# Mixture of experts after attention: a third expert's early product, early weights by columns, a later routing chain

## The chip, the cores and the metric

One core of one Trainium2 chip. The metric is the device time of one execution in microseconds, the median of repeated runs. TensorE multiplies, VectorE and ScalarE work elementwise, GpSimd issues the indirect scatters, and SyncE (SP) issues the other transfers.

## What is computed

```
q_pool = q.reshape(B, H, S // 2, 2, D).mean(axis=3)        # 4, 8, 1152, 64
attn   = softmax(q_pool @ k^T / sqrt(D));  x = attn @ v     # 2304 tokens x 512
logits = x @ w_gate;  noisy = logits + log1p(exp(x @ w_noise)) * noise
top2   = two largest of 8 experts per token, softmax weights over the two
for e in range(8):  h = relu(x[mask] @ w1[e]);  out[mask] += w * (h @ w2[e])
```

w1[e] is 512 x 1024 and w2[e] is 1024 x 512, in float32.

## The kernel before

**Precision.** Every float32 operand of the experts is split into two fp16 parts, a high and a low one, and a product is three matmuls: high by high, low by high, high by low. A 512 KB piece of a weight (four pieces for each of w1[e] and w2[e]) comes into one of four raw buffers (`qr`, `kn`, `kr`, `vr`). `split` (L907) makes the high part on ScalarE (L918) and the low part on VectorE (L920). `load` (L895) then brings the next piece into a raw buffer.

**Stages.** First comes attention, until about 446 us, in two halves of the heads' groups. Tokens of the first half are routed during it and scattered by expert into `xg` in device memory (640 rows at most are computed for each expert). Then comes the **early stage** (`Moe.early`, L1000): for experts 0 and 1 the first 256 rows, which hold tokens of the first half alone, go through both products while the second half's tokens are still being routed. Then comes the **main part** (`Moe.run`, L1049): the other 384 rows of experts 0 and 1 and all 640 of experts 2 to 7, with each expert's second product behind the next one's first. Main needs the rows of the second half, loaded from `xg` by a transposing transfer (`xload`, L925).

**The two products.** `mm1` (L956) is the first: for each of eight column blocks f, 12 matmuls of N columns (256 early, 384 or two times 320 in main) into a PSUM tile `pss`. There are two such tiles, `pss_63` and `pss_64`, and early products use a half of one each, so a pair of f shares a tile. ScalarE makes `hh` of it (L1015 early, L980 main) and VectorE the lower half `hl` (L1019, L981). `mm2` (L983) is the second: for each block of 128 rows 24 matmuls of 512 columns (L988).

**The routing chains.** For a group of three token blocks, transposed rows `xTg` are multiplied by the gate weights (logits, L693). Then a long chain of small VectorE steps on tiles `rt` and `ru` (L696 to L800) picks the two experts. A rank product on TensorE (L803 to L806) counts tokens per expert, a few VectorE steps make row addresses, and GpSimd scatters (L97). In the early stage there are two: chain C (tiles `rtc`, `ruc`) for group 0, six scatters, and chain A (`rta`, `rua`) for groups 1 and 2 together, twelve scatters.

**What sets the order.** `Plan` emits the program in the order of a simulated schedule: each operation has a key (about its due time in us), a cost, dependences and buffers, and of those that can start it takes one by start and key. `route` (L572) gives a chain's steps keys that grow by `pace`. Expert e's early work has keys from LATE + 23 e, where LATE is 440.

Of the kernel before, what the change touches and what calls it, by code (L numbers as in the profile page):

```python
# [19 lines left out]
P = 128  # L20
# [8 lines left out]
E = 8  # L29
# [7 lines left out]
NEARLY = 2  # L37

# [179 lines left out]
class Attn:  # L218
# [307 lines left out]
    def others(s, F0, out):  # L526
# [91 lines left out]
class Route:  # L618
    def __init__(s, tc, ctx, B, wg, wn, noise):
        s.tc, s.nc, s.B = tc, tc.nc, B  # L620
        nc = s.nc
        s.per = B.const
        s.rp = ctx.enter_context(tc.tile_pool(name="rt", bufs=1))
        s.wk = ctx.enter_context(tc.tile_pool(name="rwk", bufs=3))
        s.dram = ctx.enter_context(tc.tile_pool(name="rdram", bufs=1, space=DRAM))
        s.xg = s.dram.tile([E * FULL, XW], U16, name="xg")
        s.A, s.C = ("a", 9, 14, 6), ("c", 3, 18, 8)
        s.group, s.xr, s.pre = [], {}, {}
        for g in range(3):
            s.xr[1, g] = s.rp.tile([P, 3, XW], F16, name=f"xr{g}")  # L630
        s.args = wg, wn, noise
# [48 lines left out]
    def logits(s, j, g, L, gap, last):  # L680
        nc = s.nc
        xr = s.xr[j, g]
        xT = []
        for c in range(3):
            xT.append(s.rp.tile([P, 8, P], F16, name="xTg", bufs=6))
# [180 lines left out]
class Moe:  # L866
    def __init__(s, tc, ctx, B, R, F0, w1, w2, out):
# [3 lines left out]
        s.x = pool("mx", 2)  # L871
# [22 lines left out]
    def load(s, eng=None):  # L894
# [5 lines left out]
        r = s.B.flat(s.F0.raws[(s.nl - 1) % 4])  # L900
        if nm == "1":
            eng.dma_start(r, s.w1[e, c * P:(c + 1) * P])
        else:
            eng.dma_start(r.rearrange("p (a f) -> p a f", a=2),
                                s.w2[e, 2 * c * P:2 * (c + 1) * P].rearrange("(a p) f -> p a f", p=P))
        s.pre[e, nm, c] = r

    def split(s, e, nm, c, half=None, load=True):
        nc = s.nc
        if c == 0 and half != 1:  # L910
            if nm == "1" and e % 2 == 0:
# [44 lines left out]
    def mm1(s, e, f, a=0, b=CAP, ps=None):  # L956
# [3 lines left out]
        if e not in s.H:  # L960
            s.H[e] = tuple(s.h.tile([P, 8, CAP], F16, name=f"h{x}") for x in "hl")
# [41 lines left out]
    def early(s, A):  # L1003
# [4 lines left out]
        s.W[0, "1"] = s.F0.w  # L1008
        fl, ld, done = {}, {}, {}
# [15 lines left out]
        for x, (e, nm) in enumerate(((0, "2"), (1, "1"), (1, "2"))):  # L1025
            for c in range(4):
                key = LATE + (2, 12, 24)[x] + (2, 2.5, 2.5)[x] * c
                hi = op("ACT", 1.06, key, lambda e=e, nm=nm, c=c: s.split(e, nm, c, 0), deps=[ld[x, c]] if x else ())
                lo = op("DVE", 1.14, key, lambda e=e, nm=nm, c=c: s.split(e, nm, c, 1, False), deps=[hi])
                last = ld[x + 1, c] = op("SP", 0.6, key, s.load, deps=[lo], lat=5.0, after=last)  # L1030
                done.setdefault((e, nm), []).append(lo)
# [17 lines left out]
    def run(s):  # L1049
        s.nc.gpsimd.tensor_copy(s.B.sp, s.X[0, EARLY][0:1, 7, CAP - EARLY - 1:CAP - EARLY])  # L1050
        s.put()
        for e in range(E + 1):
            if e < E:
                s.meta(e, EARLY if e < NEARLY else 0, CAP)
                for f in range(8):
                    s.mm1(e, f, EARLY if e < NEARLY else 0, CAP)
                    s.flush()
                    if 1 <= e < E - 1:
                        s.split(e + 1, "1", f // 2, f % 2)
                if 1 <= e < E - 1:  # L1060
                    s.xload(e + 1, 0, CAP)
# [150 lines left out]
```

## Time and profile before

| | before |
|---|---|
| median of 3 runs | 891.49 us (889.52 to 892.16) |
| profiled execution | 896.5 us, span 894.6 us |
| mean granted TensorE clock | 0.962 |
| TensorE matmul busy | 819.0 us (92%) |
| VectorE / ScalarE / GpSimd busy | 534.6 / 445.0 / 402.6 us |
| DMA, whole span | 137.80 MB, mean 154 GB/s |

The profile is of one execution, 5.0 us longer than the median of the runs; its span leaves out 1.9 us around it. Matmuls are pipelined: a matmul's own duration is longer than the distance to the next one, so throughput is read from starts and counts. The granted clock is the share of TensorE's full clock that it was given.

### The profile page before, as it was taken

The page shows a single profiled execution, that of the slowest core. Times are in us where ns is not written, and L with a number is a line of the kernel's source. Part 1 is how long each engine was busy: PE and PEld are TensorE (multiplying, and loading weights), DVE is VectorE, ACT ScalarE, POOL GpSimd, SP SyncE. Part 2 cuts the span into 40 slices and gives each one's busy share as a digit, 9 for nine tenths or more (in the row PEclk, how much of TensorE's full clock was granted, in tenths as well). Part 3 has the DMA queues.
Part 4 walks back from the last instruction along what each step waited for, and adds up shares of the span by engine and source line. Part 5 has one row for each costly group of instructions (what it writes and reads, how often), then busy time and mean ns, then how long its engine had stood idle before and what let it go on. Part 6 is the DMA issues. An engine that isn't in the chain of part 4 may idle for free.

```text
span 894.6 us, 21128 instructions
## 1 busy us (share of the span) xinstructions
PE 819.0 (92%) x8685; PEld 537.1 (60%) x8685; DVE 534.6 (60%) x1226; ACT 445.0 (50%) x662; POOL 402.6 (45%) x389
## 2 busy tenths in 40 slices
PE   3889999999999877899988899999999999999995
PEld 1546777767767655677766365756475655647542
DVE  4877898899889988899887142434233241422200
ACT  4658888777878465586543132333233232322310
POOL 4447879887996867664633312020201102020222
PEclk9989999999999779899989899999999999999998
DMA  8899796898999587664586826282827346291143
GB/s 194 166 238 211 181 231 176 200 200 194 194 214 203 116 183 189 169 172 110 122 215 231 205 55 147 82 214 71 217 68 201 84 126 158 72 219 18 24 52 45
DMA packets 213637, 137.80 MB, mean 154 GB/s; under 512 B 150304, under 2 KB 183584, under 8 KB 213536
## 3 DMA queue, kind: packets, MB, share of 16 engines
q1 hardware_dynamic: 204896, 116.33, 53.6%
q0 software_dynamic: 8640, 20.08, 11.0%
q8 instruction: 69, 1.13, 0.5%
q14 instruction: 32, 0.26, 0.1%
HBM read 62.14 MB, written 35.44 MB: 109 GB/s over the span
## 4 chain that ended last, share of the span: by engine, by line
PE 64%; DVE 20%; issue 4%; ACT 4%; DMA 3%; another core or an unknown queue 1%; SPq 1%; POOL 1%; ACTq 0%; DVEq 0%; POOLq 0%
PE pss L971 23%; PE psm L988 21%; PE psm L385 7%; PE psm L304 5%; PE pss L350 4%; DVE pl L362 4%; PE pss L349 4%; DVE rd L318 3%; DVE kd L298 1%; ACT rd L312 1%; ACT pf L357 1%; DVE vv L288 1%; DVE mx L327 1%; DMA qt<-qn 1%
## 5 line engine op out<-in xcount | busy, mean ns | idle before, releaser
L365 POOL TENSOR_TENSOR pl<-pf 128x384 f16<-128x384 f32 x288 | 279.9, 1002 | 95.6 <-ACT pf L357 70.9
L357 ACT ACTIVATE pf<-pss 128x768 f32<-128x768 f32 x216 | 174.2, 813 | 72.1 <-PE pss L350 59.1
L97 POOL DMA_INDIRECT out_dram<-y,mti x40 | 62.2, 1554 | 317.4 <-ACT y L993 311.8
L385 PEld LDWEIGHTS <-pf 128*128 128x128 bf16 x2880 | 159.6, 99 | 52.8 <-issue 23.7
L385 PE MATMUL psm<-vv,pf 128*128 128x65 f16 (+1 forms) x2880 | 169.9, 196 | 6.0 <-ACT rd L312 3.2
L385 PE MATMUL psm<-vv,pl 128*128 128x65 f16 (+1 forms) x1440 | 161.1, 195 | 4.5 <-DVE pl L362 2.9
L349 PE MATMUL pss<-qt,kt 128*128 128x384 f16 (+1 forms) x576 | 152.1, 293 | 5.6 <-ACT pf L357 5.4
L350 PE MATMUL pss<-qt,kt 66*128 66x384 f16 (+1 forms) x576 | 152.6, 294 | 0.4 <-DMA qt<-qn 0.4
L981 DVE SCALAR_TENSOR_TENSOR hl<-pss,hh 128x640 f16<-128x640 f32 (+1 forms) x64 | 48.5, 758 | 158.9 <-ACT hh L980 158.9
L385 PEld LDWEIGHTS <-pl 128*128 128x128 f16 x1440 | 128.6, 100 | 6.1 <-DVE pl L362 3.4
L988 PE MATMUL psm<-wh,hh 128*128 128x512 f16 x320 | 122.5, 383 | 3.8 <-ACT hh L1015 3.8
L988 PE MATMUL psm<-wh,hl 128*128 128x512 f16 x320 | 122.3, 382 | 0.5 <-issue 0.5
L988 PE MATMUL psm<-wl,hh 128*128 128x512 f16 x320 | 122.5, 383 | 0.1
L318 DVE CUSTOM_DVE_ANT_0 rd<-psm,rd 128x512 f32<-128x512 f32 x144 | 97.3, 684 | 25.4 <-ACT rd L312 21.0
L988 PEld LDWEIGHTS <-hh 128*128 128x128 f16 x640 | 62.9, 98 | 79.8 <-ACT hh L1015 4.6
L993 ACT ACTIVATE y<-psm,mg 128x512 f32<-128x512 f32 x40 | 27.5, 688 | 152.0 <-issue 77.3
L980 ACT ACTIVATE hh<-pss 128x640 f16<-128x640 f32 (+1 forms) x64 | 41.7, 652 | 122.9 <-PE pss L971 122.9
L312 ACT ACTIVATE rd<-psm 128x512 f32<-128x512 f32 x144 | 85.9, 597 | 24.6 <-PE psm L304 19.7
L304 PE MATMUL psm<-kt,qt 128*128 128x512 f16 (+3 forms) x320 | 79.8, 325 | 16.4 <-DVE mx L318 8.7
L971 PE MATMUL pss<-xT,fh 128*128 128x320 f16 (+1 forms) x448 | 83.4, 303 | 0.0
L971 PE MATMUL pss<-xT,wh 128*128 128x320 f16 (+1 forms) x448 | 83.4, 303 | 0.0
L362 DVE TENSOR_TENSOR pl<-pf 128x768 f16<-128x768 f32 x72 | 82.0, 1151 | 0.2 <-ACT pf L357 0.2
(198 smaller groups left out, 1141.3 us busy)
## 6 DMA issues: line engine op xcount, KB each, us to landing
xg<-zt SPq DMA_DIRECT2D x40, 260.0 KB
kr<-in_k_dram SPq DMA_DIRECT2D x32, 288.0 KB
vr<-in_v_dram SPq DMA_DIRECT2D x16, 576.0 KB
kr<-in_moe_w_dram SPq DMA_DIRECT2D x17, 512.0 KB
qr<-in_moe_w_dram SPq DMA_DIRECT2D x16, 512.0 KB
kn<-in_moe_w_dram SPq DMA_DIRECT2D x16, 512.0 KB
qr<-in_q_dram SPq DMA_DIRECT2D x31, 256.0 KB
vr<-in_moe_w_dram SPq DMA_DIRECT2D x15, 512.0 KB
```

Of the source, the lines that this page charges most:

```text
L97: i = nc.gpsimd.indirect_dma_start(out=out, out_offset=bass.IndirectOffsetOnAxis(ap=idx, axis=0), in_=src, in_offset=None, **kw)
L304: s.nc.tensor.matmul(ps[r, o:o + m.shape[1] * P], s.G.buf["qt", i][:, c, r], m, start=True, stop=True)
L312: s.nc.scalar.activation(s.G.buf["rd", i, c], s.G.buf["D", i, c], AF.Relu)
L318: s.nc.vector.tensor_tensor_reduce(out=rd, in0=s.G.buf["S", i, c], in1=rd, scale=1.0, scalar=-3.0e38, op0=ALU.add, op1=ALU.max, accum_out= ...
L349: mm(ps[:, a, o:o + w], kt[:, hh * NK + kc, :], qf[:, q0:q0 + w], start=True, stop=False)
L350: mm(ps[:, a, o:o + w], kt2[0:66, hh * NK + kc, :], qf2[0:66, q0:q0 + w], start=False, stop=True)
L357: s.nc.scalar.activation(s.parts(u)[0], s.G.buf["ps", u][:, :, 0:SG], AF.Exp, scale=0.125 / (IN_SCALE * IN_SCALE))
L362: s.nc.vector.tensor_sub(pl, pf, ph)
L365: s.nc.gpsimd.tensor_sub(pl[:, a], pf[:, a], ph[:, a])
L385: mm(o[:, 0:x], src[:, t % 2, ci * P:ci * P + P], vv[:, hh * NK + kc, a:a + x], start=st, stop=last and src is pl, skip_group_check=True)
L971: nc.tensor.matmul(ps[:, i, 0:N], w[:, dc, f * P:(f + 1) * P], xT[:, 2 * dc + x, i * N:(i + 1) * N], start=(n == 0), stop=(n == 11))
L988: s.nc.tensor.matmul(ps, h[:, f, b * P:(b + 1) * P], w[:, f, :], start=(f == 0 and k == 0), stop=(f == 7 and k == 2))
```

## The change

- `NFIRST = 3`: expert 2's first 256 rows go through the first product in the early stage too; its second product stays in main, whose first product for expert 2 then has 384 rows.
- The w1 parts of expert 2 get a tile of their own (`w1x`), in the place of one of two `xT` buffers. The `xT` tiles of main get fixed homes in memory that the routing has finished with.
- The w1 pieces of experts 1 and 2 are loaded and split by columns (256 of 1024) instead of by rows, so that a pair of column blocks f needs one piece alone; the second product's matmuls wait for their own splits and lower halves instead of for all.
- The first two pieces of w1 of expert 1 are loaded into memory of `hl` of expert 1, without a wait for a raw buffer. Sixteen pieces are split in the early stage instead of twelve.
- Chain C gets key 440 and pace 0.3 instead of key 425, chain A LATE + 8 instead of LATE + 6.
- Rows 0 to 255 of expert 2 are loaded once (`xload(2, 0, EARLY)`), ahead of the second half's scatters.

```diff
+NFIRST = 3
...
-                s.route(R.steps(1, (1, 2), R.A, 0.3, s.half[0]), LATE + 6, [], 0.2, True, then=rows, pace=0.35, first=("DVE", 0.12))
-
-        s.route(R.steps(1, (0,), R.C, 0.3), 425, late[0], 0.2, True, then=rows)
+                s.route(R.steps(1, (1, 2), R.A, 0.3, s.half[0]), LATE + 8, [], 0.2, True, then=rows, pace=0.35, first=("DVE", 0.12))
+
+        s.route(R.steps(1, (0,), R.C, 0.3), 440, late[0], 0.2, True, then=rows, pace=0.3)
...
+        z = s.x.tile([P, 5 * F * 2], F16, name="w1x")
+        s.w1x = tuple(z[:, x * 4 * F:(x + 1) * 4 * F].rearrange("p (d f) -> p d f", d=4) for x in range(2))
...
+        s.home = {(0, EARLY): cut(late, 0, L), (1, EARLY): cut(late, 8 * L, L), (2, EARLY): cut(rows, 0, L),
+                  (2, 0): cut(z, 8 * F, EARLY)}
...
-        r = s.B.flat(s.F0.raws[(s.nl - 1) % 4])
-        if nm == "1":
+        if s.nl < 7:
+            r = s.H[1][1].rearrange("p a b -> p (a b)").bitcast(F32)[:, (s.nl - 5) * F:(s.nl - 4) * F]
+        else:
+            r = s.B.flat(s.F0.raws[(s.nl - 7) % 4])
+        if nm == "1" and e in (1, 2):
+            eng.dma_start(r.rearrange("p (d f) -> p d f", d=4),
+                          s.w1[e, :, c * 2 * P:2 * (c + 1) * P].rearrange("(d p) f -> p d f", p=P))
+        elif nm == "1":
             eng.dma_start(r, s.w1[e, c * P:(c + 1) * P])
...
+        A.xe[2] = op("SP", 1.4, LATE + 21, lambda: s.xload(2, 0, EARLY), lat=4.0)
+        for x in range(16):
+            e, nm, c = s.loads[x]
+            key = LATE + (2, 12, 24, 36)[x // 4] + (2, 2.5, 2.5, 2.5)[x // 4] * c
...
+            for y in (4, 5, 6) if x == 0 else (x + 6,) if x < 4 else (x + 4,) if x > 5 else ():
+                last = ld[y] = op("SP", 0.6, key, s.load, deps=los[x:x + 1] if y > 5 else (), lat=5.0, after=last)
...
-        for e in range(2):
-            k0 = LATE + 23 * e
+        for e in range(NFIRST):
+            k0 = LATE + (0, 23, 46)[e]
...
-                mm = op("PE", 1.28, k0 + 1.3 * f, lambda e=e, f=f: one(e, f), deps=done[e, "1"] + [A.xe[e]],
+                mm = op("PE", 1.28, k0 + 1.3 * f, lambda e=e, f=f: one(e, f), deps=(done[e, "1"][f // 2:f // 2 + 1] if e else done[e, "1"]) + [A.xe[e]],
...
-            for b in range(2):
+            for b in range(2 if e < NEARLY else 0):
...
-                            deps=lows + done[e, "2"] if q == 0 else (), take=[("bank", ("y", e, b))] if q == 0 else (), after=mm)
+                            deps=lows[2 * q:2 * q + 2] + done[e, "2"][q:q + 1] if b == 0 else (), take=[("bank", ("y", e, b))] if q == 0 else (), after=mm)
...
-                s.meta(e, EARLY if e < NEARLY else 0, CAP)
+                if e == 2:
+                    s.meta(e, 0, EARLY)
+                s.meta(e, EARLY if e < NFIRST else 0, CAP)
                 for f in range(8):
-                    s.mm1(e, f, EARLY if e < NEARLY else 0, CAP)
+                    s.mm1(e, f, EARLY if e < NFIRST else 0, CAP)
                     s.flush()
-                    if 1 <= e < E - 1:
+                    if 2 <= e < E - 1:
                         s.split(e + 1, "1", f // 2, f % 2)
```

Three places of the order show what moved; line numbers of the changed kernel are higher (L700 there is L696 before, L947 is L920, L1046 is L1019, L996 is L971, L807 is L803, L1013 is L988).

VectorE at the start of chain C, before:

```order
L696 TENSOR_SCALAR ruc<-psm_67 128x48
L726 SCALAR_TENSOR_TENSOR rtc<-ruc 128x24
L728 TENSOR_SCALAR rtc<-rtc 128x24
L731 TENSOR_SCALAR rtc<-rtc 128x24
L733 TENSOR_SCALAR rtc<-rtc 128x24
L736 SCALAR_TENSOR_TENSOR rtc<-rtc 128x24
L738 SCALAR_TENSOR_TENSOR rtc<-rtc 128x24
L740 TENSOR_SCALAR rtc<-rtc 128x24
```

and with the change:

```order
L700 TENSOR_SCALAR ruc<-psm_67 128x48
L730 SCALAR_TENSOR_TENSOR rtc<-ruc 128x24
L732 TENSOR_SCALAR rtc<-rtc 128x24
L947 SCALAR_TENSOR_TENSOR wl_8212<-qr,wh_8211 128x1024
L735 TENSOR_SCALAR rtc<-rtc 128x24
L1046 SCALAR_TENSOR_TENSOR hl<-pss_63,hh 128x256
L737 TENSOR_SCALAR rtc<-rtc 128x24
L740 SCALAR_TENSOR_TENSOR rtc<-rtc 128x24
L742 SCALAR_TENSOR_TENSOR rtc<-rtc 128x24
L744 TENSOR_SCALAR rtc<-rtc 128x24
L747 TENSOR_SCALAR rtc<-rtc 128x24
L1046 SCALAR_TENSOR_TENSOR hl<-pss_63,hh 128x256
```

Weight splits (`wl`) and lower halves (`hl`) now stand between the steps of chain C. Up to C's last step ahead of the rank product there are four splits, eight lower halves and fourteen steps of groups 1 and 2 that stood behind it before.

TensorE around chain A's rank product (`rua`), before, where it stands between the two experts' early work:

```order
L988 LDWEIGHTS hh
L988 MATMUL psm_66<-wl_8223,hh 128x512
L988 LDWEIGHTS hl
L988 MATMUL psm_66<-wh_8222,hl 128x512
L803 LDWEIGHTS tri
L803 MATMUL psm_65<-rua,tri 128x56
L805 LDWEIGHTS ones
L805 MATMUL psm_65<-rua,ones 128x48
```

and with the change:

```order
L996 LDWEIGHTS wh_8434
L996 MATMUL pss_64<-xe_7364,wh_8434 128x256
L996 LDWEIGHTS wl_8435
L996 MATMUL pss_64<-xe_7364,wl_8435 128x256
L807 LDWEIGHTS tri
L807 MATMUL psm_65<-rua,tri 128x56
L809 LDWEIGHTS ones
L809 MATMUL psm_65<-rua,ones 128x48
```

It now stands in the midst of expert 1's first product, behind 36 of its matmuls. C's rank product stands in expert 0's second product, behind 18 matmuls of it, where it stood in the first one, behind 60.

TensorE at the end of the early stage, before (`xT` is the rows of main, the matmul of 384 columns its first):

```order
L988 MATMUL psm_67<-wl_8648,hh 128x512
L988 LDWEIGHTS hl
L988 MATMUL psm_67<-wh_8647,hl 128x512
L971 LDWEIGHTS fh
L971 MATMUL pss_64<-xT,fh 128x384
```

and with the change:

```order
L996 LDWEIGHTS w1x
L996 MATMUL pss_64<-w1x 128x256
L996 LDWEIGHTS fh
L996 MATMUL pss_64<-xTg,fh 128x384
L996 LDWEIGHTS fh
```

Expert 2's product is now the last of the early stage, and its last matmuls write the PSUM tile `pss_64` that main's first matmul writes too.

## Rows read from the trace of the kernel before

**Rows 1.** Busy time by engine, granted clock, DMA share, GB/s: the main part

```profile
core 0: us, PE busy (x) PEld busy (x) DVE busy (x) ACT busy (x) POOL busy (x), PEclk, DMA share, GB/s
...
509.50:883.70 374.20, 374.15 (x2208) 215.84 (x2206) 110.00 (x170) 111.87 (x148) 58.69 (x38) 1.00 0.47 111
```

**Rows 2.** TensorE's timeline, early stage: start, duration, instruction, idle before it and releaser

```profile
446.76 0.38 PE L971 MATMUL pss<-xe,fh 128*128 128x256 f16 x2
...
452.00 0.17 PE L693 MATMUL psm<-wh,xTg 128*128 128x16 f16 x1
...
452.90 0.38 PE L971 MATMUL pss<-xe,fh 128*128 128x256 f16 x2
...
456.30 0.18 PE L803 MATMUL psm<-ruc,tri 128*128 128x32 f16 x1 [1.92 <-DVE ruc L800]
...
458.90 0.61 PE L971 MATMUL pss<-xe,fh 128*128 128x256 f16 x2 [1.46 <-DVE hl L1019]
...
478.79 0.21 PE L803 MATMUL psm<-rua,tri 128*128 128x56 f16 x1 [2.50 <-DVE rua L800]
...
499.92 0.61 PE L988 MATMUL psm<-wh,hh 128*128 128x512 f16 x1 [3.79 <-ACT hh L1015]
...
509.33 0.49 PE L971 MATMUL pss<-xT,fh 128*128 128x384 f16 x2
```

**Rows 3.** TensorE alone, stretches of one matmul form: 384, 512, 320 columns

```profile
core 0: us, PE busy (x), PEclk, DMA share, GB/s
510.00:525.00 15.00, 15.00 (x94) 1.00 0.50 68
541.00:555.00 14.00, 14.00 (x67) 1.00 0.80 179
557.00:582.00 25.00, 25.00 (x186) 1.00 0.26 74
```

**Rows 4.** The early stage by stretches of granted clock, columns as in rows 1

```profile
446.80:458.10 11.30, 8.72 (x141) 7.78 (x137) 9.50 (x59) 6.13 (x11) 0.00 (x0) 1.00 0.79 122
458.10:465.00 6.90, 6.10 (x30) 4.34 (x31) 6.58 (x21) 0.39 (x1) 5.29 (x4) 0.51 0.75 246
478.50:482.10 3.60, 3.31 (x23) 2.43 (x23) 3.58 (x19) 1.32 (x2) 0.25 (x1) 0.53 0.59 215
482.10:499.00 16.90, 13.37 (x101) 9.49 (x98) 6.67 (x18) 4.20 (x8) 12.18 (x12) 1.00 0.94 325
499.00:506.00 7.00, 6.08 (x15) 2.11 (x16) 0.85 (x2) 1.46 (x3) 0.00 (x0) 0.51 0.55 125
```

**Rows 5.** ScalarE's and VectorE's timelines: evacuation of expert 1's first and last pair

```profile
483.26 0.38 ACT L1015 ACTIVATE hh<-pss 128x256 f16<-128x256 f32 x1 [3.44 <-PE pss L971]
...
499.48 0.38 ACT L1015 ACTIVATE hh<-pss 128x256 f16<-128x256 f32 x1 [7.36 <-remote]
...
499.90 0.43 DVE L1019 SCALAR_TENSOR_TENSOR hl<-pss,hh 128x256 f16<-128x256 f32 x1 [6.73 <-ACT hh L1015]
...
500.36 0.38 ACT L1015 ACTIVATE hh<-pss 128x256 f16<-128x256 f32 x1 [0.49 <-DVE hl L1019]
...
500.77 0.42 DVE L1019 SCALAR_TENSOR_TENSOR hl<-pss,hh 128x256 f16<-128x256 f32 x1 [0.45 <-ACT hh L1015]
```

**Rows 6.** VectorE's timeline: start of chain C, a split, a lower half

```profile
447.55 0.20 DVE L696 TENSOR_SCALAR ruc<-psm 128x48 f32<-128x48 f32 x1
...
456.16 1.22 DVE L920 SCALAR_TENSOR_TENSOR wl<-qr,wh 128x1024 f16<-128x1024 f32 x1
...
457.30 0.16 DVE L809 TENSOR_SCALAR rtc<-rtc 128x3 f32<-128x3 f32 x1
...
466.65 0.42 DVE L1019 SCALAR_TENSOR_TENSOR hl<-pss,hh 128x256 f16<-128x256 f32 x1 [1.66 <-ACT hh L1015]
...
467.00 0.18 DVE L743 TENSOR_SCALAR rta<-rta 128x48 f32<-128x48 f32 x1
```

**Rows 7.** GpSimd's and SP's timelines: first of chain A's scatters, main's rows issued, landed

```profile
481.85 1.41 POOL L97 DMA_INDIRECT xg<-xr,rta  x1 [14.01 <-DVE xr L835]
...
501.31 2.91 SPq L928 DMA_TRANSPOSE xT<-xg  x1
...
506.55 0.18 POOL L1050 CAST sp<-xT 1x1 f32<-1x1 f16 x1 [8.92 <-DMA xT<-xg]
```

More of the change, by code (lines that the diff above doesn't have):

```diff
@@ L628, in __init__ @@
         s.group, s.xr, s.pre = [], {}, {}
+        s.tok2 = s.rp.tile([P, 9, XW], F16, name="xr")
         for g in range(3):
-            s.xr[1, g] = s.rp.tile([P, 3, XW], F16, name=f"xr{g}")
+            s.xr[1, g] = s.tok2[:, 3 * g:3 * g + 3]
+        s.xTg, s.nx = s.rp.tile([P, 6, 8, P], F16, name="xTg"), 0
         s.args = wg, wn, noise
@@ L684, in logits @@
         for c in range(3):
-            xT.append(s.rp.tile([P, 8, P], F16, name="xTg", bufs=6))
+            xT.append(s.xTg[:, s.nx % 6])
+            s.nx += 1
             nc.sync.dma_start_transpose(out=xT[c], in_=xr[:, c, 0:2 * DM])
@@ L889, in __init__ @@
             s.X[e, 0], s.G[e, 0] = R.pre[e]
+        z = s.x.tile([P, 5 * F * 2], F16, name="w1x")
+        s.w1x = tuple(z[:, x * 4 * F:(x + 1) * 4 * F].rearrange("p (d f) -> p d f", d=4) for x in range(2))
+        late = R.xTg.rearrange("p c d r -> p (c d r)")
+        rows = R.tok2.rearrange("p c m -> p (c m)")
+        cut = lambda t, a, n: t[:, a:a + 8 * n].rearrange("p (d r) -> p d r", d=8)
+        L = CAP - EARLY
+        s.home = {(0, EARLY): cut(late, 0, L), (1, EARLY): cut(late, 8 * L, L), (2, EARLY): cut(rows, 0, L),
+                  (2, 0): cut(z, 8 * F, EARLY)}
+        for e in range(3, E):
+            s.home[e, 0] = cut(rows, 8 * L, CAP) if e % 2 else cut(z, 0, CAP)
         s.nl = 4
@@ L910, in split @@
         if c == 0 and half != 1:
-            if nm == "1" and e % 2 == 0:
+            if (e, nm) == (2, "1"):
+                s.W[e, nm] = s.w1x
+            elif nm == "1" and e % 2 == 0:
                 s.W[e, nm] = s.F0.w
@@ L916, in split @@
         r = s.pre[e, nm, c]
+        if nm == "1" and e in (1, 2):
+            r = r.rearrange("p (d f) -> p d f", d=4)
+            hi, lo = (t[:, :, c * 2 * P:2 * (c + 1) * P] for t in (hi, lo))
+        else:
+            hi, lo = hi[:, c], lo[:, c]
         if half != 1:
-            nc.scalar.activation(hi[:, c], r, AF.Copy, scale=WS)
+            nc.scalar.activation(hi, r, AF.Copy, scale=WS)
         if half != 0:
-            nc.vector.scalar_tensor_tensor(lo[:, c], r, WS, hi[:, c], op0=ALU.mult, op1=ALU.subtract)
+            nc.vector.scalar_tensor_tensor(lo, r, WS, hi, op0=ALU.mult, op1=ALU.subtract)
             if load:
@@ L925, in xload @@
         nc = s.nc
-        s.X[e, a] = s.x.tile([P, 8, CAP], F16, name="xT")
+        s.X[e, a] = s.home[e, a]
         rows = s.R.xg[e * FULL + a:e * FULL + b]
-        nc.sync.dma_start_transpose(out=s.X[e, a][:, :, 0:b - a], in_=rows[:, 0:2 * DM].bitcast(F16))
+        nc.sync.dma_start_transpose(out=s.X[e, a], in_=rows[:, 0:2 * DM].bitcast(F16))
         n = (b - a) // P
@@ L959, in mm1 @@
         xT = s.X[e, a]
-        if e not in s.H:
-            s.H[e] = tuple(s.h.tile([P, 8, CAP], F16, name=f"h{x}") for x in "hl")
         hh, hl = s.H[e]
@@ L1008, in early @@
         s.W[0, "1"] = s.F0.w
+        for e in range(E):
+            s.H[e] = s.H[e % 2] if e > 1 else tuple(s.h.tile([P, 8, CAP], F16, name=f"h{x}") for x in "hl")
         fl, ld, done = {}, {}, {}
@@ L1023, in one @@
             fl[e, f] = s.late.pop()
[L1025 to L1031, printed above, removed]
+        los = []
+        A.xe[2] = op("SP", 1.4, LATE + 21, lambda: s.xload(2, 0, EARLY), lat=4.0)
+        for x in range(16):
+            e, nm, c = s.loads[x]
+            key = LATE + (2, 12, 24, 36)[x // 4] + (2, 2.5, 2.5, 2.5)[x // 4] * c
+            hi = op("ACT", 1.06, key, lambda e=e, nm=nm, c=c: s.split(e, nm, c, 0), deps=[ld[x]] if x in ld else ())
+            los.append(op("DVE", 1.14, key, lambda e=e, nm=nm, c=c: s.split(e, nm, c, 1, False), deps=[hi]))
+            for y in (4, 5, 6) if x == 0 else (x + 6,) if x < 4 else (x + 4,) if x > 5 else ():
+                last = ld[y] = op("SP", 0.6, key, s.load, deps=los[x:x + 1] if y > 5 else (), lat=5.0, after=last)
+            done.setdefault((e, nm), []).append(los[-1])
         done[0, "1"] = [A.f0]
-        for e in range(2):
-            k0 = LATE + 23 * e
+        for e in range(NFIRST):
+            k0 = LATE + (0, 23, 46)[e]
             mm, lows = None, []
-            mt = op("DVE", 0.8, k0 + 16, lambda e=e: s.meta(e, 0, EARLY), deps=[A.xe[e]])
+            if e < NEARLY:
+                mt = op("DVE", 0.8, k0 + 16, lambda e=e: s.meta(e, 0, EARLY), deps=[A.xe[e]])
             for f in range(8):
-                mm = op("PE", 1.28, k0 + 1.3 * f, lambda e=e, f=f: one(e, f), deps=done[e, "1"] + [A.xe[e]],
+                mm = op("PE", 1.28, k0 + 1.3 * f, lambda e=e, f=f: one(e, f), deps=(done[e, "1"][f // 2:f // 2 + 1] if e else done[e, "1"]) + [A.xe[e]],
                         take=[("half", ("m", e, f))], after=mm)
```

4 lines of the change are left out of this document (2 added, 2 removed).

## The prediction

> **What bounds the kernel now.** I first read the whole span by slices and then by stage. From 509.50 to 883.70 us TensorE is busy for 374.15 of 374.20 us at a granted clock of 1.00 [rows 1]: the main part is bound by the matmuls themselves, and nothing that VectorE, ScalarE or a queue does there costs time. The change leaves attention, before 446 us, in the same order on every engine. So the time can only be found in the early stage between them, and every microsecond by which that stage ends sooner, with the same matmuls done, is a microsecond of the result.
>
> The second view is TensorE's timeline of that stage, which names what ended each idle stretch [rows 2]. The stage begins at 446.76 us and the main part's first matmul starts at 509.33: 62.57 us. At full clock its work is much shorter. Forty-eight 256-column matmuls take 452.00 - 446.76 = 5.24 us, 0.109 each, so 192 of them take 21.0. A 512-column matmul is 14 us over 65 (two of the 67 counted straddle an edge of the window), 0.215 [rows 3], so 96 take 20.7. One group's logits take 0.90 us (452.00 to 452.90) and there are two more groups: 1.8. The rank products take some 0.3. Together 43.8 us, so 18.8 us are lost.
>
> Where they are lost is in two views. TensorE's four idle stretches are 1.92 us for chain C's last VectorE step (`ruc`), 1.46 for a lower half `hl` that chain C holds up, 2.50 for chain A's (`rua`), and 3.79 for `hh` of expert 1: 9.7 us [rows 2]. The granted clock fell to the lower of its two levels (1.2 of 2.4 GHz) in three stretches, each at or right behind such an idle: 0.51 over 6.90 us, 0.53 over 3.60 and 0.51 over 7.00 [rows 4]. What they cost is the share not granted: 3.4 + 1.7 + 3.4 = 8.5 us. 9.7 and 8.5 explain 18.2 of the 18.8.
>
> The last idle is odd: the `hh` that ended it waited 7.36 us for something that the profile calls remote [rows 5], and not for a matmul as the `hh` at 483.26 did. The DMA engines were 0.94 busy at 325 GB/s then [rows 4]. I call this the late completion; with the half clock behind it, it costs 3.79 + 3.43 = 7.2 us.
>
> **The change part by part.** *Expert 2's early product.* It brings 96 matmuls of 256 columns into the stage, 96 x 0.109 = 10.5 us, and takes them out of the main part. There expert 2's first product was 192 of 320 columns, 25 us over 184 = 0.136 each, 26.1 us; it becomes 96 of 384 columns at 15 over 92 = 0.163, 15.6 us [rows 3]. 10.5 against 10.5: the move costs and gives nothing by itself. What it gives is work that TensorE can do while others finish, so I go through the idles.
>
> *`hl`, 1.46 us.* The next pair's matmuls waited for a PSUM tile whose lower half stood behind chain C on VectorE. Now the lower halves stand between C's steps, so I put this idle at 0; what they take from C is in the next term.
>
> *`ruc`, 1.92 us.* TensorE now comes to C's rank product after 96 x 0.109 + 1.8 + 18 x 0.215 = 16.2 us, at 463.0. VectorE has to do more before it. Chain C took from 447.55 to 456.30, with one lower half in it [rows 6]: 8.75 - 0.35 = 8.4 us. New in between are four weight splits at 457.30 - 456.16 = 1.14 us (4.6), eight lower halves at 467.00 - 466.65 = 0.35 us (2.8) and fourteen small steps of the later groups, 0 to 2.4 us as they fill the waits of C's chain or not. That is 447.55 + 15.8 to 18.2 = 463.3 to 465.7. I take 464.0, so 1.0 us idle; the ends are 0 and 1.92, the present row.
>
> *`rua`, 2.50 us.* TensorE comes to A's rank product after C's with 30 x 0.215 + 36 x 0.109 = 10.4 us of work, at 474.4. VectorE has four splits (4.6) and what is left of chain A: from 467.00 to 478.79 it took 11.8 us with three splits in it [rows 2, 6], 8.4 without them; some five of these steps now come before C's rank product, so about 7.3. The tail of C and the meta steps of expert 0, some twenty small ones, are 0 to 1.8 more. That makes 11.9 to 13.7 after 464.0, so idle of 1.5 to 3.3. I take 2.0, nearer the lower end because such steps fill the waits of A's chain.
>
> *The late completion, 3.79 us.* TensorE has expert 2's product to do in this stretch, but it stands behind expert 1's second product in order, so it would not cover the wait. I still put it at 0: it stands once in the trace, and the profiled execution was 5.0 us above the median of the runs, which would fit a stall of 7.2 us that the others mostly lack. It is the largest term without proof; it comes back as a rival.
>
> *A new wait at the boundary.* Main's first matmul writes PSUM tile `pss_64`, and so does the last early pair, now directly ahead of it. Before, 48 matmuls of the second product stood between. The last pair must first be evacuated: `hh`, `hl`, `hh`, `hl` in a row, 499.48 to 501.19 in the trace [rows 5], 1.71 us and two hand-overs, so 1.9 us. The first `hh` of a pair started at 483.26, after both halves [rows 5], so the pair is not overlapped. The lower end is one `hh` and one `hl`, 0.9.
>
> *The clock.* Idle of 1.92 us was still followed by a clock of 1.00 up to 458.10 [rows 4]; the fall came with the next idle. The 2.50 was followed by 3.60 us at half. For my 2.0 at `rua` and the 1.9 at the boundary I take such a short stretch each, 1.7 us; the ends are 0 and 3.4. The Trainium skill's page "TensorE: Matmul & The Clock Gate", Part 1, says that for modelling the ramp is under 1% of a typical span and not worth fitting. By that rule the clock's gain of 8.5 - 3.4 = 5.1 us would be left out and the result would be 891.1; the row says half clock for 17.5 us in this stage alone, so I keep it.
>
> *Loads, splits, queues.* Splitting by columns keeps 128x1024 elements for each split, so its 1.22 us stays [rows 6]. ScalarE has room: it is busy for 4.20 of 16.90 us [rows 4]. SP issues four more 512 KB loads (2.1 MB) and expert 2's rows (0.27 MB) ahead of the main part's rows: 2.4 MB, 7.3 us at 325 GB/s [rows 4]. They are hidden while main's rows land before TensorE needs them. In the trace these were issued 22.5 us after A's rank product, behind the twelve scatters, and were there 27.8 us after it, at 506.55 [rows 2, 7]. TensorE now has 60 x 0.109 + 48 x 0.215 + 96 x 0.109 = 27.3 us of work from the same point, and with the clock and the boundary 31: a margin of 3.1 us.
>
> **The sum.** Left over are 1.0 + 2.0 + 1.7 + 1.9 + 1.7 = 8.3 of 18.8 us, a gain of 10.5. The profiled execution took 896.5 us, so 886.0. The runs' median, 891.49, is 5.0 below the execution that this is made against; I do not subtract it again, since the late completion that may explain it is already taken out. With all low ends (0, 1.5, 0, 0.9, 0) it is 880.1; with all high ends (1.9, 3.3, 3.4, 1.9, 3.4) 891.6.
>
> **The rivals.**
> *Main's rows come late.* For it: the margin of 3.1 us is small and the DMA engines are 0.94 busy under the scatters. Against: over 499 to 506 they are at 0.55. If all 7.3 us of the new transfers push in front, main waits 4.2 us longer and may run long enough at half clock to lose 3.4 more: 893.6, no change. The Trainium skill, "DMA: Bandwidth & Descriptors", section "Issuing engines are not separate DMA queues", says that transfers of SP and GpSimd run on the same 16 engines and interleave, which is this mechanism. Chance 0.07.
> *The clock is worth nothing here*, as the page's rule has it, 891.1: against it stand three rows [rows 4]. 0.05.
> *The late completion stays, once*: 886.0 + 7.2 = 893.2. 0.04.
> *Slower: the late completion comes twice.* Place: the evacuations of expert 1's and expert 2's pairs, now both under the twelve scatters and more loads than before. Each costs 7.2 us, and from two on (14.4) the gain is eaten: 900.4. For it: it fell where the DMA was busiest. Against: one stretch of the trace only. 0.08.
> *That the change does not do what it says* is excluded by the order shown above.
>
> **How the numbers follow.** A measurement here can tell about 0.3%, 2.7 us: faster means under 888.8. My forecast and its low side have 0.76 (about 0.1 of it is that the 5.0 us are the profiler's own and the runs end near 881), no change 0.07 + 0.05 + 0.04 = 0.16, slower 0.08. The range goes from 879.0, the low end and a part of the 5.0 us, to 891.6, the sum of the high ends.
>
> **What would show it.** Right: no TensorE wait for `hl` in expert 0's first product; the idle for `ruc` near 1 and for `rua` near 2 us; a wait of about 1.9 us for `hl` at the main part's first matmul; main starting near 509 us although it is 10.5 us shorter; low clock under 8 us in all. Wrong: a wait of main's first matmul for its rows or of a pair of expert 2 for its split, a second `hh` that waits for something remote, or half clock well into the main part.

## The result and the profile after

| | before | after |
|---|---|---|
| median of the runs | 891.83 us (889.52 to 893.68, 4 runs) | 882.76 us (879.36 to 884.49, 4 runs) |
| ratio | | 0.9895, interval 0.9864 to 0.9927 |
| profiled execution, span | 896.5, 894.6 us | 879.36, 877.4 us |
| stage begins, main starts | 446.76, 509.33 us | 442.70, 502.68 us |
| early stage | 62.57 us | 59.98 us |
| TensorE work in it at full clock | 43.8 us | 54.3 us |
| lost in it | 18.8 us | 5.7 us |

The change makes the kernel 9.1 us faster, 1.05%, against a forecast of 886.0 us (5.5 us faster). The two profiled executions are 17.1 us apart. 4.1 us of that is in attention, where nothing changed (the early stage simply begins sooner, 442.70 against 446.76), 2.6 us in the early stage, and 10.4 us in the main part, which gave matmuls to the early stage. "Stage" is in all that follows the time from expert 0's first early matmul to main's first matmul. "Work at full clock" is the prediction's 43.8 us, and 10.5 more with the change; "lost" is the rest of the stage.

TensorE's timeline of the early stage after the change, the lines that answer to [rows 2]:

```profile
442.70 0.38 PE L996 MATMUL pss<-xe,fh 128*128 128x256 f16 x2
...
459.28 0.18 PE L807 MATMUL psm<-ruc,tri 128*128 128x32 f16 x1 [0.24 <-DVE ruc L804]
...
471.29 0.19 PE L807 MATMUL psm<-rua,tri 128*128 128x56 f16 x1 [1.34 <-DVE rua L804]
...
473.88 0.38 PE L996 MATMUL pss<-xe,wh 128*128 128x256 f16 x2 [0.95 <-DVE hl L1046]
...
502.68 0.50 PE L996 MATMUL pss<-xTg,fh 128*128 128x384 f16 x2 [2.55 <-DMA xTg<-xg]
```

These are all its waits: 0.24 + 1.34 + 0.95 + 2.55 = 5.1 us, where they were 9.7. The last one is new: main's first matmul waits for a DMA, the transposed rows of expert 0. The wait for `hh` of 3.79 us is gone.

The same stage and the main part by stretches, columns as in [rows 1, 4]:

```profile
core 0: us, PE busy (x) PEld busy (x) DVE busy (x) ACT busy (x) POOL busy (x), PEclk, DMA share, GB/s
442.70:458.00 15.30, 15.30 (x188) 12.56 (x185) 13.58 (x60) 10.12 (x16) 0.00 (x0) 1.00 1.09 236
458.00:482.00 24.00, 21.46 (x156) 14.33 (x155) 22.32 (x110) 11.25 (x19) 13.09 (x11) 1.00 0.80 263
482.00:502.60 20.60, 18.12 (x132) 12.65 (x130) 8.09 (x20) 6.55 (x12) 8.68 (x8) 1.00 0.86 293
502.60:866.40 363.80, 363.72 (x2112) 206.61 (x2112) 104.86 (x182) 105.51 (x143) 60.74 (x40) 1.00 0.50 109
```

The granted clock is 1.00 from the stage's beginning on; not one of the stage's idles was followed by the lower level. The main part is as gapless as before and 374.15 - 363.72 = 10.4 us shorter: expert 2's moved matmuls. VectorE is the busiest of the others (13.58 of 15.30 us, 22.32 of 24.00).

How main's rows came, in SP's and GpSimd's timelines, as in [rows 7]: the last load ahead of them, the last scatter, the rows issued, the rows there.

```profile
488.04 0.33 SPq L922 DMA_DIRECT2D kn<-in_moe_w_dram  x1
...
491.84 0.97 POOL L98 DMA_INDIRECT xg<-xr,rta  x1 [0.30 <-issue]
...
497.72 2.90 SPq L955 DMA_TRANSPOSE xTg<-xg  x1
...
502.69 0.18 POOL L1081 CAST sp<-xTg 1x1 f32<-1x1 f16 x1 [9.88 <-DMA xTg<-xg]
```

The rows are there 59.99 us after the stage began, the same instant at which TensorE goes on. In [rows 7] it was 506.55 - 446.76 = 59.79 us. The evacuation of the last early pair, ScalarE and VectorE:

```profile
500.22 0.38 ACT L1042 ACTIVATE hh<-pss 128x256 f16<-128x256 f32 x1 [1.36 <-PE pss L996]
...
500.64 0.42 DVE L1046 SCALAR_TENSOR_TENSOR hl<-pss,hh 128x256 f16<-128x256 f32 x1 [1.32 <-ACT hh L1042]
...
501.09 0.38 ACT L1042 ACTIVATE hh<-pss 128x256 f16<-128x256 f32 x1 [0.49 <-DVE hl L1046]
...
501.51 0.42 DVE L1046 SCALAR_TENSOR_TENSOR hl<-pss,hh 128x256 f16<-128x256 f32 x1 [0.45 <-ACT hh L1042]
```

It ends at 501.93, 0.75 us ahead of the rows: the wait that I had forecast for the boundary is there, under another one.

### The profile page after: what moved, and what is told of

Read it like the earlier page. It is cut to its first block, busy times and chain, and to the rows that moved or that the text cites. A ratio compares the mean times of both kernels' runs of the same rounds, so it can differ in the third digit from the quotient of the medians.

```text
span 877.4 us, 21164 instructions
## 1 busy us (share of the span) xinstructions
PE 805.1 (92%) x8685; PEld 531.6 (61%) x8685; DVE 533.7 (61%) x1242; ACT 445.5 (51%) x670; POOL 403.0 (46%) x389
## 4 chain that ended last, share of the span: by engine, by line
PE 67%; DVE 21%; issue 4%; ACT 3%; DMA 3%; SPq 1%; POOL 1%; ACTq 0%; DVEq 0%; POOLq 0%
PE pss L996 23%; PE psm L1013 22%; PE psm L386 8%; PE psm L305 6%; PE pss L351 4%; PE pss L350 4%; DVE pl L363 3%; DVE rd L319 3%; DVE kd L299 1%; DVE vv L289 1%; ACT rd L313 1%; DVE mx L328 1%; ACT pf L358 1%; DMA kr<-in_k_dram 1%; DVE kn L289 1%
## 5 line engine op out<-in xcount | busy, mean ns | idle before, releaser
L386 PEld LDWEIGHTS <-pf 128*128 128x128 bf16 x2880 | 157.7, 98 | 51.8 <-issue 21.9
L386 PE MATMUL psm<-vv,pf 128*128 128x65 f16 (+1 forms) x2880 | 168.0, 195 | 5.1 <-ACT rd L313 3.5
L386 PE MATMUL psm<-vv,pl 128*128 128x65 f16 (+1 forms) x1440 | 159.2, 194 | 4.5 <-DVE pl L363 3.0
L1006 DVE SCALAR_TENSOR_TENSOR hl<-pss,hh 128x640 f16<-128x640 f32 (+1 forms) x64 | 46.3, 724 | 161.7 <-ACT hh L1005 161.7
L1013 PE MATMUL psm<-wl,hh 128*128 128x512 f16 x320 | 121.3, 379 | 0.0
L1013 PE MATMUL psm<-wh,hl 128*128 128x512 f16 x320 | 121.3, 379 | 0.0
L1013 PE MATMUL psm<-wh,hh 128*128 128x512 f16 x320 | 121.3, 379 | 0.0
L1013 PEld LDWEIGHTS <-hh 128*128 128x128 f16 x640 | 62.6, 98 | 73.8
L1005 ACT ACTIVATE hh<-pss 128x640 f16<-128x640 f32 (+1 forms) x64 | 39.9, 623 | 119.9 <-PE pss L996 119.9
L305 PE MATMUL psm<-kt,qt 128*128 128x512 f16 (+3 forms) x320 | 78.2, 317 | 19.2 <-DVE mx L319 10.3
L363 DVE TENSOR_TENSOR pl<-pf 128x768 f16<-128x768 f32 x72 | 79.1, 1111 | 0.1
L305 PE MATMUL psm<-kd,qt 128*128 128x512 f16 (+1 forms) x160 | 58.5, 405 | 20.4 <-DVE kd L299 10.0
L305 PEld LDWEIGHTS <-qt 128*128 128x128 f16 (+1 forms) x480 | 37.4, 102 | 61.8 <-issue 41.5
```

Of the source, the lines that this page charges most:

```text
L305: s.nc.tensor.matmul(ps[r, o:o + m.shape[1] * P], s.G.buf["qt", i][:, c, r], m, start=True, stop=True)
L363: s.nc.vector.tensor_sub(pl, pf, ph)
L386: mm(o[:, 0:x], src[:, t % 2, ci * P:ci * P + P], vv[:, hh * NK + kc, a:a + x], start=st, stop=last and src is pl, skip_group_check=True)
L1013: s.nc.tensor.matmul(ps, h[:, f, b * P:(b + 1) * P], w[:, f, :], start=(f == 0 and k == 0), stop=(f == 7 and k == 2))
```

## The theories and the experiments

That the rows land at the same distance from the stage's beginning in both profiles suggests a theory that the prediction lacks. **ROWS**: main can't start before its rows are scattered, read back and transposed, and in these two profiles that is some 60 us after the stage's beginning. The change does not shorten that; it puts 10.5 us of main's work under it. (The equal distance is two shifts that cancel: chain A's rank product, behind which its scatters and then the rows come, comes 28.59 us after the stage's beginning instead of 32.03, and the rows land 31.4 us behind it instead of 27.8. In the runs below they land 56.5 to 62.8 us after the beginning.) The rival **CHAINS** lets the gain come from the interleaved chains and the split by columns, which take TensorE's idles away. **STALL** has the late completion of the first profile in every execution, so that a large part of the gain is its absence. Ratios are to the kernel before on the same chip; the numbers of the changed kernel are 882.76 us above and 884.2 in the fifth run.

**1. The kernel before, once more** (no edit).

> The kernel before, unchanged, profiled a second time. Theory ROWS: the late completion of the first profile (3.79 us of idle for hh, 7.2 us with its half clock) is a single event. Without it TensorE is through with the early work some 55 us after the stage begins, and then main waits for its rows, which land 59.8 us after the beginning (506.55 - 446.76): the idle for hh is under 1 us, a wait of 3 to 5 us for the transposed rows stands before main's first matmul, and the stage is 59.5 to 60.5 us long. Theory STALL: the late completion is in every execution; the idle for hh is 3 to 4 us again and the stage 62 to 63 us. Both: 891.8 us, within 0.3%.

Measured: 892.44 us, ratio 0.9997 (0.998 to 1.0014). TensorE's timeline of it, rank product A and main's first matmul:

```profile
475.40 0.19 PE L803 MATMUL psm<-rua,tri 128*128 128x56 f16 x1 [2.50 <-DVE rua L800]
...
501.69 0.80 PE L971 MATMUL pss<-xT,fh 128*128 128x384 f16 x2 [5.04 <-DMA xT<-xg]
```

TensorE does not wait for `hh`; in its place it waits 5.04 us for the rows. The stage began at 443.68 and took 58.01 us. Late signals there are in this execution too, on ScalarE:

```profile
488.76 0.39 ACT L1015 ACTIVATE hh<-pss 128x256 f16<-128x256 f32 x1 [3.79 <-remote]
...
495.92 1.46 ACT L993 ACTIVATE y<-psm,mg 128x512 f32<-128x512 f32 x2 [5.89 <-remote]
```

They hit other results, which TensorE did not need yet, and so held nothing up. The two stretches of lower clock and the one after, columns as above:

```profile
454.40:461.20 6.80, 5.39 (x26) 3.83 (x27) 6.57 (x24) 0.38 (x1) 4.28 (x5) 0.50 0.81 251
...
498.80:505.60 6.80, 3.91 (x13) 1.84 (x13) 0.78 (x8) 0.00 (x0) 3.05 (x3) 0.50 1.10 213
505.60:520.00 14.40, 14.40 (x90) 8.64 (x89) 3.98 (x8) 3.93 (x8) 3.44 (x3) 1.00 0.67 71
```

The second one takes in the first 3.91 us of main, at half speed: 2.0 us. STALL, which has the wait for `hh` in every execution, falls: late signals do recur in the kernel before, but they need not hold TensorE, and here, where they don't, TensorE waits for the rows instead.

The first profile's 5.0 us above the median can now be laid out against this one, which ran near it: 446.76 - 443.68 = 3.1 us later at the beginning of the stage, 62.57 - 58.01 = 4.6 us in it, and 2.0 us less in main's beginning. That is 5.7 us, the spans' difference (894.6 - 888.9).

**2. Expert 2's early product moved back into main** (all else as changed).

```diff
-        for e in range(NFIRST):
+        for e in range(NEARLY):
             k0 = LATE + (0, 23, 46)[e]
...
                 s.meta(e, EARLY if e < NFIRST else 0, CAP)
+                if e == 2:
+                    for f in range(8):
+                        s.mm1(e, f, 0, EARLY)
+                        s.flush()
```

> The changed kernel, but expert 2's early product is moved back to the main part (same 96 matmuls of 256 columns, put ahead of its other 384 rows); loads, splits by columns, buffers and later chains stay. Theory ROWS: main still starts when its rows land, 60 us after the stage begins, and the 10.5 us of expert 2 come on top: 882.8 + 10.5 = 893 (891 to 895), with a wait of 10 us or more for the rows ahead of main. Theory CHAINS (the gain comes from the later, interleaved chains and the split by columns): 882.8 within 3 us, main starting 8 to 10 us sooner.

Measured: 894.88 us, ratio 1.0032 (1.002 to 1.0043): 10 to 12 us slower than the changed kernel, and even a little slower than the kernel before. Main's first matmul:

```profile
504.93 0.48 PE L996 MATMUL pss<-xTg,fh 128*128 128x384 f16 x1 [13.03 <-DMA xTg<-xg]
```

13.03 us of waiting, which is 10.5 + 2.5. The stage (from 444.90) is 60.03 us, as long as with the moved work in it. That is what ROWS says, and CHAINS falls: chains, columns, buffers and early loads without the moved work bring nothing. One cost comes on top, which ROWS did not have: behind the long wait main begins at the lower clock (columns as above).

```profile
504.93:510.70 5.77, 5.77 (x19) 2.66 (x19) 1.37 (x9) 0.49 (x1) 3.38 (x3) 0.50 1.24 173
```

Half of 5.77 us is 2.9; with the 10.5 us of work it explains the 13.4 us by which this execution is longer than the changed one from the stage's beginning to the end of the span (448.1 against 434.7 us).

**3. The old keys of both chains in the changed kernel.**

```diff
-                s.route(R.steps(1, (1, 2), R.A, 0.3, s.half[0]), LATE + 8, [], 0.2, True, then=rows, pace=0.35, first=("DVE", 0.12))
+                s.route(R.steps(1, (1, 2), R.A, 0.3, s.half[0]), LATE + 6, [], 0.2, True, then=rows, pace=0.35, first=("DVE", 0.12))
...
-        s.route(R.steps(1, (0,), R.C, 0.3), 440, late[0], 0.2, True, then=rows, pace=0.3)
+        s.route(R.steps(1, (0,), R.C, 0.3), 425, late[0], 0.2, True, then=rows)
```

> The changed kernel with the keys of both routing chains put back (425 and LATE + 6, no pace for chain C). Theory ROWS: the rows land at about the same time, but the idles for ruc and hl are back (1.9 + 1.5 us and up to 3.4 us of half clock), so TensorE's early work ends 57.4 + 3 to 7 us after the beginning and sets main's start instead of the rows: 883 to 887. Theory CHAINS: the later chains are most of the gain: 888 or more. If neither matters: 882.8 within 1 us.

Measured: 885.14 us, ratio 0.9932 (0.9908 to 0.9956). TensorE again, with GpSimd's line for the rows between:

```profile
455.40 0.61 PE L996 MATMUL pss<-xe,fh 128*128 128x256 f16 x2 [1.43 <-DVE hl L1046]
...
506.07 0.18 POOL L1081 CAST sp<-xTg 1x1 f32<-1x1 f16 x1 [9.24 <-DMA xTg<-xg]
...
507.81 0.48 PE L996 MATMUL pss<-xTg,fh 128*128 128x384 f16 x2 [1.86 <-DVE hl L1046]
```

The idles of the old order are back (1.91 us for `ruc` just ahead of the 1.43) with a lower clock behind them, the stage (from 443.28) is 64.53 us, and what main waits for last is `hl`, not the rows. The rows did not land at about the same time, as expected, but 62.79 us after the beginning, 2.8 later: chain A's rank product came only 32.78 us after it, so TensorE's and VectorE's order ahead of that does move the rows. With more work in the stage TensorE's idles do count, 4.5 us of stage in this profile. The time shows some 1 to 3 us (ratio 0.9932 against 0.9895 and 0.9917), and the intervals overlap; it is more than in the kernel before, as the next run shows.

**4. The new keys alone, in the kernel before** (the reverse edit).

> The kernel before with nothing but the new keys of the two chains (440 with pace 0.3, LATE + 8). Theory ROWS: the idles for ruc and hl go (3.4 us), but main waits for its rows instead, which land as late as before or 1 to 2 us later: 891.8 to 894. Theory CHAINS: 885 to 889. If the first profile's stall is in every execution (theory STALL): 888 to 890.

Measured: 891.04 us, ratio 0.9979 (0.9965 to 0.9993). Main's first matmul:

```profile
502.11 0.80 PE L971 MATMUL pss<-xT,fh 128*128 128x384 f16 x2 [6.40 <-DMA xT<-xg]
```

TensorE's waits for `hl` and `rua` are nearly gone (1.45 and 2.50 us in run 1), `ruc` has 2.84, and what is saved is waited for again ahead of main, 6.40 us where it was 5.04. All waits of the stage together are 10.3 us against 10.9. The rows came after 56.54 us (the stage began at 445.57), 1.5 sooner than in run 1 and not later as I expected, since chain A's rank product came 3.0 us sooner (28.74 us after the beginning instead of 31.72). Of these 1.5 us main loses 0.8 again, as it runs 5.59 us at the lower clock here (502.11 to 507.70) and 3.91 in run 1. The time gains 0.2%.

**5. The changed kernel, once more** (no edit).

> The changed kernel, unchanged, profiled a second time beside the next three. Theory ROWS: main's first matmul waits 2 to 3 us for its rows again, which land 59.5 to 60.5 us after the stage begins; 882.8 us within 1.5.

Measured: 884.2 us, ratio 0.9917 (0.9894 to 0.994). The rows are waited for 2.48 us, the stage is 504.69 - 444.79 = 59.90 us. The same picture a second time. But both profiled executions of the change are the fastest of their four and six, 3.4 and 2.8 us below the medians, and so is that of run 7 (879.57 against 884.59). What the slower ones lose, and where, no profile shows: attention, which ends up to 5 us apart, can be a part of it, and a lower clock behind the wait for the rows, as behind the 2.42 us of run 9, is a candidate that was not tested.

**6. Expert 3's loads behind main's rows.**

```diff
-            for y in (4, 5, 6) if x == 0 else (x + 6,) if x < 4 else (x + 4,) if x > 5 else ():
+            for y in (4, 5, 6) if x == 0 else (x + 6,) if x < 4 else (x + 4,) if 5 < x < 12 else ():
...
         s.put()
+        for c in range(4):
+            s.load()
         for e in range(E + 1):
```

> The changed kernel with the four loads of expert 3's first weight (2.1 MB) issued by SP behind main's first rows instead of ahead of them. Theory DMA (these loads share the DMA engines with the last scatters, so that main's rows are issued 5.9 us after the last scatter starts, where the kernel before had 3.3 in its second profile): the rows are issued 3 to 4 us after the last scatter and land 56 to 57 us after the stage begins. The wait of main's first matmul for them goes, but the wait for the lower half hl of the last early pair takes its place: idle 1.9 instead of 2.55 us, so 0.3 to 1 us faster than the changed kernel. Rival (the rows wait for GpSimd and the routing chain alone): rows at 60 us as before, same time.

Measured: 881.1 us, ratio 0.989 (0.9861 to 0.9919). Last scatter, rows issued, rows there, and main's first matmul (the stage began at 441.70):

```profile
492.38 0.97 POOL L98 DMA_INDIRECT xg<-xr,rta  x1 [0.31 <-issue]
...
495.19 3.04 SPq L955 DMA_TRANSPOSE xTg<-xg  x1
...
500.35 0.18 POOL L1081 CAST sp<-xTg 1x1 f32<-1x1 f16 x1 [7.00 <-DMA xTg<-xg]
...
501.06 0.48 PE L996 MATMUL pss<-xTg,fh 128*128 128x384 f16 x2 [1.87 <-DVE hl L1046]
```

From the last scatter to the issue of the rows it is 2.81 us instead of 5.88, and 2.81 again in run 8; in the other profiles with these loads ahead it is 4.8 to 6.5. So the four loads do hold the last scatters up. The rows land after 58.65 us, 1.3 sooner. I had expected 3, but the last scatter itself started 1.5 us later (50.68 us after the beginning against 49.14). Main then waits for `hl`, 1.87 us, the boundary wait of the prediction, whose size was 1.9. The stage gains 0.6 us. The medians are 3.1 us apart (881.1 against 884.2), with intervals that overlap; this profile does not account for that.

**7. Main's first product in the other PSUM tile.**

```diff
         s.put()
+        s.B.wide()
         for e in range(E + 1):
```

> The changed kernel with main's first product in the other PSUM tile, so that it does not have to wait for the last early pair's evacuation; loads as in the change. Theory ROWS: the wait for the rows stands in front of main anyway: 882.8 within 1 us, the same as the changed kernel. If the evacuation is what holds main: 1.9 us faster.

Measured: 884.59 us, ratio 0.992 (0.9899 to 0.9941), the same as the changed kernel. Main still waits for the rows, 2.40 us:

```profile
502.89 0.50 PE L996 MATMUL pss<-xTg,fh 128*128 128x384 f16 x2 [2.40 <-DMA xTg<-xg]
```

Taking away a wait that lies under another was worth nothing here.

**8. Both edits together.**

> Both edits together. Theory DMA with ROWS: main's first matmul waits for neither rows nor hl; TensorE goes from the last early matmul into main without idle, 57.4 us after the stage begins, 2.5 us faster than the changed kernel: about 880.3. If one of the two edits does not do what it should, 0 to 1 us faster.

Measured: 880.17 us, ratio 0.9858 (0.9833 to 0.9884), against 884.2 for the changed kernel in the same comparison. The stage began at 446.19, and main's first matmul stands in the timeline with no wait:

```profile
503.44 0.49 PE L996 MATMUL pss<-xTg,fh 128*128 128x384 f16 x2
```

57.25 us, 2.7 less than the 59.98 and 59.90 of the change, where neither edit alone gave over 0.6 of the stage. The rows are there 0.26 us ahead of main (503.18). That it takes both edits is shown by the stage and its waits; in the medians run 6 alone has 3.1 of the 4.0 us. In run 11 the same kernel had 878.98 us, ratio 0.9866 (0.9837 to 0.9895). It is the best version found, some 3 to 4 us below the change.

**9. The split by rows again.**

```diff
-        if nm == "1" and e in (1, 2):
+        if False:
...
-                mm = op("PE", 1.28, k0 + 1.3 * f, lambda e=e, f=f: one(e, f), deps=(done[e, "1"][f // 2:f // 2 + 1] if e else done[e, "1"]) + [A.xe[e]],
+                mm = op("PE", 1.28, k0 + 1.3 * f, lambda e=e, f=f: one(e, f), deps=done[e, "1"] + [A.xe[e]],
```

> The changed kernel with the first weight of experts 1 and 2 loaded and split by rows again, so that the first matmul of each needs all four splits instead of one. Theory COLUMNS matters: TensorE comes to expert 1 some 23 us after the stage begins and the fourth split ends some 27 us after it: 4 us of idle there, of which 2.3 come back at the idles for rua and hl that stand later; TensorE's early work ends 59 us after the beginning, and with the 1.9 us of evacuation main starts at 61 instead of 60, 1 us slower than the changed kernel (0.5 to 4.5 with half clock behind the idle): 884 to 887. Rival (main's rows set its start whatever TensorE does before): 883.5 within 1 us. Expert 2 should not be held up in either case, its last split ends before TensorE comes to it.

Measured: 886.02 us, ratio 0.9946 (0.9928 to 0.9964), some 2 to 4 us slower than the change (ratios 0.9917 and 0.9895), where I had expected 1 (0.5 to 4.5). TensorE's wait for the last split of expert 1, and main's first matmul:

```profile
472.36 0.40 PE L996 MATMUL pss<-xe,wl 128*128 128x256 f16 x1 [2.42 <-DVE wl L947]
...
509.25 0.49 PE L996 MATMUL pss<-xTg,fh 128*128 128x384 f16 x2 [1.86 <-DVE hl L1046]
```

The wait is there, smaller than my 4 us, with a lower clock behind it for 6.8 us from 471.6. The stage (from 445.11) is 64.14 us and main waits for `hl`, while the rows have been there since 506.58: TensorE sets its start. So the columns are a part of the gain, as they let TensorE be done by the time that the rows are.

**10. Chain A ahead of the splits**, in the kernel of run 8.

```diff
-                s.route(R.steps(1, (1, 2), R.A, 0.3, s.half[0]), LATE + 8, [], 0.2, True, then=rows, pace=0.35, first=("DVE", 0.12))
+                s.route(R.steps(1, (1, 2), R.A, 0.3, s.half[0]), LATE + 8, [], 0.2, True, then=rows, pace=0.2, first=("DVE", 0.12))
```

> The kernel with both edits of the eighth run (loads of expert 3 behind main's rows, main in the other PSUM tile) and chain A's pace 0.2 instead of 0.35, which puts its steps ahead of splits. There TensorE is idle for 0.24 + 1.33 + 0.95 us in the early stage and nothing waits at main. Expected: the idle for rua goes from 1.3 to under 0.5 us, the stage from 57.25 to 55.5 to 56.5 us, 1 us faster than the eighth run. Rival: the splits that chain A passes come late for expert 1's matmuls and the idle moves there: the same time.

Measured: 881.53 us, ratio 0.9906 (0.9875 to 0.9936); run 11 beside it 878.98. The idle grew instead of going:

```profile
471.12 0.21 PE L807 MATMUL psm<-rua,tri 128*128 128x56 f16 x1 [2.95 <-DVE rua L804]
...
504.16 0.49 PE L996 MATMUL pss<-xTg,fh 128*128 128x384 f16 x2
```

The idle for `rua` is 2.95 us instead of 1.43. The planner, with chain A due sooner, also put A's rank product 24 matmuls sooner into TensorE's order, so TensorE came to it sooner and waited longer; and the clock was at the lower level for 6.8 us behind it. The stage (from 443.95) is 60.21 us against 57.38 in run 11.

**11. The kernel of run 8, once more**, a reference for run 10.

> The eighth run's kernel a second time, as a reference for the tenth: about 880.5, the stage 57 to 57.5 us, no idle ahead of main.

Measured: 878.98 us, ratio 0.9866 (0.9837 to 0.9895). No wait ahead of main; the stage is 504.28 - 446.90 = 57.38 us.

## Why the prediction was right, and where it was not

The direction and the range hold, and so does the idea that the moved work fills time in which TensorE would wait: 10.5 us were moved into the early stage, and run 2 shows that without them there is no gain. Which wait they fill was not foreseen. Of the signs of being wrong that the prediction names, one came: main's first matmul waits for its rows, and not for `hl`. The time came 3.2 us lower than the forecast. By its own steps:

- *Expert 2's early product*, 10.5 against 10.5: right, the main part is 10.4 us shorter. "Gives nothing by itself" was wrong: it is the gain. Against run 1 the 2.0 us by which the stage got longer and the 2.0 us of half clock that main no longer has cancel.
- *`hl`*, 0: right for expert 0, but one of 0.95 us came at expert 1, where a lower half stands behind a split; not foreseen.
- *`ruc`*, 1.0: 0.24. *`rua`*, 2.0: 1.34. TensorE came when I had said, 16.3 us after the stage's beginning. VectorE was sooner: chain C took 15.8 us from its first step at 443.49, where I had 15.8 to 18.2, and chain A 12.0 behind it (11.9 to 13.7), both the ends at which the small steps fill the waits of the chains.
- *The late completion*, 0: right that the stall of TensorE is no part of every execution (run 1), though late signals are. Wrong in what its absence is worth: I subtracted 7.2 us as if TensorE could go on at once. Without it the stage is 4.6 us shorter and then waits for the rows, with 2.0 us of half clock into main.
- *The boundary*, 1.9 us for `hl`: measured 1.87 (run 6) and 1.86 (run 3), but in the change it lies under the 2.55 for the rows. The rival of late rows had a margin of 3.1 us; the rows came 502.69 - 471.29 = 31.4 us after A's rank product instead of 27.8, so the margin was used up and 0.5 us more. That rival happened, at a small fraction of its price: main waits 2.55 us where it would have waited 1.9 for `hl`, and the clock did not fall.
- *The clock*, 1.7 + 1.7 us left: 0. This is more than the difference of 8.3 to 5.7 us lost; the idles and what no wait explains go the other way. The 8.5 us that it took for the kernel before holds idle time that is in the 9.7 too; by the busy time in those rows it is 7.5. In run 1 it is half of 5.39 and 3.91 busy us, 4.7 us. But only the 2.0 of them that lie in main lengthen the time there, as the others stand ahead of the 5.04 us wait for the rows. The Trainium skill ("TensorE: Matmul & The Clock Gate", Part 1) puts the ramp's penalty under 1% of a typical span and advises against fitting a count of slow matmuls. The trace agrees: 4.7 us are 0.5% of run 1's span, though the 2.0 in main are still a fifth of this change's gain.
- *The sum.* The step that failed is the base. I took all of the 18.8 us lost in one execution for something that TensorE could win back by having work. But main had two conditions, TensorE's own work and its rows, and I used the second only as a margin of the changed kernel, not as what bounds the kernel before. Against run 1 the stage goes from 58.01 to 59.98 us with 10.5 us more work in it and 2.0 us of half clock less behind it: 10.5 us net. The medians moved by 9.1. That my sum was 10.5 too is chance, of other terms, and was set against an execution that is 5.0 us above the median. From the median of the runs, 10.5 us less are 881.0, nearer to the measured 882.76.

On the rival "Main's rows come late": with four loads of SP among GpSimd's last scatters the rows are issued 5.88 us after the last scatter started, without them 2.81 (run 6). The Trainium skill ("DMA: Bandwidth & Descriptors", section "Issuing engines are not separate DMA queues") has transfers of both engines interleave on the same 16 DMA engines; the trace agrees.

## What to carry to other kernels

Where a stage is bounded by a chain that ends in memory traffic, find the time at which that chain can end at the earliest, and look for work from behind it to fill the stage: shortening TensorE's other waits gave next to nothing (0.2%, run 4) before the stage was full, and then they counted (runs 3 and 9). An idle's releaser names only the last of several waits; of two at one place, removing either alone left the other (runs 6 to 8). And where the profiled execution is longer than the median, profile the same kernel once more before summing against it.

## What was not expected of the hardware

- **Idles of the same length were followed by the lower clock in one execution and not in another.** 2.50 us at the same instruction of the same kernel: 3.6 us at 0.53 in the first profile of before, 1.00 in the second. Of 2.40, 2.48 and 2.55 ahead of main none was, the 2.42 of run 9 was. In or behind the longer ones of the stage (2.84, 2.95, 3.79, 5.04, 6.40 and 13.03) it fell each time.
- **TensorE results were signalled late**, under the scatters of chain A, in all three profiles of kernels with the old early order. ScalarE waited 2.77 and 7.36 us in the first of before (where it cost TensorE 3.79), 3.79 and 5.89 in the second, and 6.6 in run 4. The last matmul of the pair that was waited for 7.36 us had ended at 491.09, 8.4 us before `hh` began. None of the other ten profiles has a wait for something remote in that stage. Which part of the change does it stays open: the new keys alone did not take the late signals away (run 4), and neither the old keys (run 3), nor the split by rows (run 9), nor expert 2 in main (run 2) brought them back; the buffers, the earlier loads and the fixed homes were not tried alone.
- **Attention ends up to 5 us apart**, though up to the stage's beginning every engine has the same instructions in the same order in all thirteen profiles: the stage began between 441.70 and 446.90 us in the profiles, and between 443.68 and 446.76 in the two of the kernel before. Stages are better compared from their own beginning than from the start of the program.
